# Where the last k features are computed in the prologue of a polysketch attention and squared-ReLU FFN kernel

## Chip, cores, metric

One NeuronCore of a Trainium2 chip. The metric is the device time of one execution in microseconds. Executions come in two states: most agree within 0.3%, a few are 2 to 3.3% longer ("slow").

## The reference, cut to what matters

```python
def phi(x):                                   # per token: 8 x 8 products of two sketches
    a = einsum('rd,bhsd->bhsr', S1, x)        # r = 8, head_dim 32
    b = einsum('rd,bhsd->bhsr', S2, x)
    return einsum('bhsi,bhsj->bhsij', a, b).reshape(..., 64)
q_p, k_p = phi(q), phi(k)                     # batch 4, heads 4, seq 1088
kv  = einsum('bhsf,bhsd->bhfd', k_p, v)
z   = sum(k_p, axis=2)
out = (q_p @ kv) / (q_p . z + 1e-6)           # then x = out as 4352 tokens x 128
h   = relu(x @ w_in)                          # 128 -> 2048
y   = (h * h) @ w_out                         # 2048 -> 128
```

Everything is fp32. The FFN is the bulk of the work. The attention of each batch must be done before that batch's FFN may start, and for the first batch nothing is there to hide it behind. That is the prologue.

## The kernel before

For the first batch the keys are cut into nine tiles of 128 tokens (0 to 8). Each tile goes through three engines:

- `kf`: TensorE computes both sketches of a tile (one matmul per tile, 64 columns) into a PSUM bank;
- `kb`: ScalarE copies one half of it to SBUF;
- `kp`: VectorE multiplies the halves (one instruction per group of tiles);
- `kvp`: TensorE multiplies kp by v and adds up over the tiles (four matmuls per tile, one per head).

The q features of the first 256 tokens take the same way: two sketches `q0(0)` and `q0(1)` on TensorE, the copy `qb` on ScalarE, the product `qp0` on VectorE. When kvp is complete VectorE makes the block `bd` from it, and then den and num (the denominator and the numerator of `out`) and the first FFN input xT follow, after which the FFN matmuls begin.

```python
    def a_kf(t0, n, pool, tag):
        kf = pool.tile([128, 512], F32, tag=tag, name="kf")     # each tag: a ring of two PSUM banks
        for t in range(n):
            nc.tensor.matmul(_ap(kf, 0, 128, 32 * t, [[32 * n, 2], [1, 32]]),
                             kt0[:, 128 * (t0 + t) : 128 * (t0 + t) + 128], sf[:, 0:64])
        kb = wpool.tile([128, 32 * 3], F32, tag="kb", bufs=4, name="kb")
        nc.scalar.copy(kb[:, 0 : 32 * n], kf[:, 32 * n : 64 * n])
        st["kf", t0] = kf, kb
    # ... (a_kp0: one tensor_tensor of kf and kb; a_kv0: four matmuls, 128 rows, 64 columns)
    def q0(x):
        for y in range(2):                                       # two halves of 64 rows
            r, o = slice(64 * y, 64 * y + 64), 512 * (2 * x + y)
            nc.tensor.matmul(x0[:, o : o + 256], sq[r, 128 * x : 128 * x + 128], qT[r, 0:256])
    # ...
    a_kf(0, 2, psf, "po")
    a_kf(2, 2, psf, "pg")
    a_kf(4, 3, psf, "po")
    q0(0)
    q0(1)
    nc.scalar.copy(_ap(qb0, ...), banks(x0, 0, 0, 256))
    st[0, "kvp"] = psf.tile([128, 512], F32, tag="pg", name="kvp")
    for t0, n in ((0, 2), (2, 2), (4, 3), (7, 2)):
        a_kp0(t0, n)
        for t in range(t0, t0 + n):
            a_kv0(t)
        if t0 == 0:
            a_kf(7, 2, psf, "po")
    nc.vector.tensor_tensor(out=_ap(qp0, ...), in0=banks(x0, 2, 0, 256), in1=_ap(qb0, ...), op=mult)
    # ... den0 (eps), bd, kvt, num0, reciprocal, xT, then the FFN
```

Of the kernel before, what the change touches and what calls it, by code (L numbers as in the profile page):

```python
# [14 lines left out]
def _ap(t: bass.AP, p0: int, np_: int, off: int, free):  # L15
    p = list(t.ap)[0]
    return bass.AP(
        t.tensor, t.offset + p0 * p[0] + off, [[p[0], np_]] + [list(d) for d in free]
    )
# [85 lines left out]
def kernel(  # L105
# [43 lines left out]
    psf = ctx.enter_context(tc.tile_pool(name="psf", bufs=2, space=bass.MemoryType.PSUM))  # L149
# [122 lines left out]
    def banks(t_, x, col, n, k=2):  # L272

        return _ap(t_, 0, 128, 512 * x + col, [[512, k], [1, n]])
# [28 lines left out]
    def a_kf(t0, n, pool, tag):  # L303
        kf = pool.tile([128, 512], F32, tag=tag, name="kf")
        for t in range(n):
            nc.tensor.matmul(  # L306
                _ap(kf, 0, 128, 32 * t, [[32 * n, 2], [1, 32]]),
                kt0[:, 128 * (t0 + t) : 128 * (t0 + t) + 128],
                sf[:, 0:64],
# [4 lines that stand above are left out]
# [5 lines left out]
    def a_kp0(t0, n):  # L319

        kf, kb = st["kf", t0]
        nc.vector.tensor_tensor(
            out=_ap(st[0, "kp"], 0, 128, 256 * t0, [[64, 4 * n], [8, 8], [1, 8]]),
            in0=_ap(kf, 0, 128, 0, [[8, 4 * n], [1, 8], [0, 8]]),
            in1=_ap(kb, 0, 128, 0, [[8, 4 * n], [0, 8], [1, 8]]),
            op=mult,
        )
# [45 lines left out]
    def a_kv0(t):  # L373
        for h in range(H):
            i, y, o, o_v = h % 2, h // 2, 64 * (H * t + h), 32 * (NT * h + t)
            nc.tensor.matmul(  # L376
                st[0, "kvp"][64 * i : 64 * i + 64, 64 * y : 64 * y + 64],
                st[0, "kp"][:, o : o + 64],
                _ap(vn[0], 0, 128, o_v, [[VC - o_v, 2], [1, 32]]),
                start=(t == 0 and y == 0),  # L380
                stop=(t == NT - 1),
                skip_group_check=True,
            )
# [362 lines left out]
    def q0(x):  # L746
        for y in range(2):
            r, o = slice(64 * y, 64 * y + 64), 512 * (2 * x + y)
            nc.tensor.matmul(x0[:, o : o + 256], sq[r, 128 * x : 128 * x + 128], qT[r, 0:256])  # L749
# [5 lines left out]
    a_kf(2, 2, psf, "pg")  # L755
    a_kf(4, 3, psf, "po")
    q0(0)
    q0(1)
    nc.scalar.copy(_ap(qb0, 0, 128, 0, [[256, 2], [1, 256]]), banks(x0, 0, 0, 256))
    st[0, "kvp"] = psf.tile([128, 512], F32, tag="pg", name="kvp")  # L760
    for t0, n in ((0, 2), (2, 2), (4, 3), (7, 2)):
        a_kp0(t0, n)
        for t in range(t0, t0 + n):
            a_kv0(t)
        if t0 == 0:
            a_kf(7, 2, psf, "po")
    nc.vector.tensor_tensor(
        out=_ap(qp0, 0, 128, 0, [[256, 2], [1, 256]]), in0=banks(x0, 2, 0, 256),
        in1=_ap(qb0, 0, 128, 0, [[256, 2], [1, 256]]), op=mult,
# [229 lines left out]
    for u in range(NU):  # L999
# [38 lines left out]
        if d0 + m == NB and (b, ci) != (B - 1, last):  # L1038
            po = [x for u_ in range(first_unit[b, c0], u + 1) for x in pe2[u_]]
# [48 lines left out]
```

## Time and profile before

| | before |
|---|---|
| fast runs | 189.06, 189.63 and, profiled, 189.23 us (a fourth, 195.55, was slow) |
| span of the profiled core | 187.4 us |
| first FFN matmul starts | 14.17 us |

Here is the timeline of TensorE in the prologue: start, length, engine (PE is TensorE, PEld its weight loads, DVE VectorE, ACT ScalarE), line, operation, output and inputs, count. TensorE executes in order and the modelled lengths overlap a little, so the cost of a piece is read from its start to the start of the next.

```profile
5.32 1.75 PE L306 MATMUL kf<-sf,kt 128*128 128x64 f32 x14
7.00 1.13 PE L749 MATMUL x<-qT,sq 64*128 64x256 f32 x8
8.06 0.69 PE L376 MATMUL kvp<-vn,kp 128*64 128x64 f32 x16
8.68 0.66 PE L306 MATMUL kf<-sf,kt 128*128 128x64 f32 x4
9.27 1.85 PE L376 MATMUL kvp<-vn,kp 128*64 128x64 f32 x56
11.05 0.65 PE L773 MATMUL den<-eps 1*64 1x256 f32 x4
```

From start to start: both q sketches 1.06 us (7.00 to 8.06), kvp of tiles 0 and 1 0.62, the late kf 0.59, the other kvp 1.78. The sum, from the first sketch to the first den matmul, is 4.05 us. I call this **the stretch**. Every fp32 matmul of this stretch has two records in the trace.

### The profile page before, as it was taken

To read this page: it belongs to the slowest core of one execution; us is meant where nothing else is said; L and a number is where in the kernel's file an instruction comes from. 1 tells how busy PE (TensorE), PEld (TensorE's weight loads), DVE (VectorE), ACT (ScalarE), POOL (GpSimd) and SP (SyncE) were. 2 spreads that over 40 slices of the span, in tenths; PEclk is the share of its full clock that TensorE was granted. 3 is DMA by queue.
4 is the path that set the end of the run, shared out by engine and by line. 5 is a ranking of instruction groups with operands and counts; after the bars stand their busy time and mean duration, and the time that the engine had idled before them with its cause. 6 is when DMAs were issued, how large, how long until landed. Compare 5 with 4: busy or idle time off the path is not lost.

```text
span 187.4 us, 4142 instructions
## 1 busy us (share of the span) xinstructions
PE 182.0 (97%) x1586; PEld 121.8 (65%) x1587; DVE 115.0 (61%) x261; ACT 149.4 (80%) x329; POOL 28.0 (15%) x125
## 2 busy tenths in 40 slices
PE   8999999999999999999999999999999999999991
PEld 2757866666656666656577666656577655666890
DVE  4779879958992589469944589469943412222400
ACT  3418778778978989789698989789698998999960
POOL 2832000028400000085000000085000000000000
PEclk9999999999999999999999999999999999999998
DMA  6799400100039600200069200200020200020101
GB/s 189 189 344 325 125 3 2 28 3 5 0 50 251 143 6 0 44 1 2 7 146 251 35 3 0 42 3 0 7 41 0 35 0 2 9 43 0 31 11 28
DMA packets 24411, 11.27 MB, mean 60 GB/s; under 512 B 17864, under 2 KB 22728, under 8 KB 24392
## 3 DMA queue, kind: packets, MB, share of 16 engines
q1 hardware_dynamic: 23940, 10.82, 23.7%
q8 instruction: 12, 0.20, 0.4%
q10 hardware_dynamic: 452, 0.20, 0.4%
q14 instruction: 7, 0.06, 0.1%
HBM read 8.78 MB, written 2.23 MB: 59 GB/s over the span
## 4 chain that ended last, share of the span: by engine, by line
PE 94%; DMA 2%; DVE 1%; issue 0%; ACT 0%; POOL 0%; ACTq 0%; DVEq 0%
PE po L653 60%; PE pg L615 18%; PE nd L538 3%; PE kvp L394 2%; PE pol L648 2%; PE po L648 2%; PE qc L296 2%; DMA s_nat<-in_S_dram 2%; PE kvp L376 1%; PE kf L306 1%; PE kc L296 1%; PE x L749 1%; PE nd L547 1%; PE den L795 0%; PE den L773 0%
## 5 line engine op out<-in xcount | busy, mean ns | idle before, releaser
L653 PE MATMUL po<-g,w_o 128*128 128x384 f32 (+3 forms) x352 | 138.4, 478 | 0.0
L615 PE MATMUL pg<-xT,w_in 128*128 128x384 f32 (+3 forms) x192 | 110.1, 582 | 0.3 <-DVE xT L810 0.3
L624 ACT ACTIVATE gt<-pg 128x384 f32<-128x384 f32 (+4 forms) x177 | 85.2, 489 | 20.0 <-PE pg L615 16.9
L653 PEld LDWEIGHTS po<-g,w_o 128*128 128x128 f32 x352 | 62.6, 189 | 22.3 <-issue 7.3
L632 ACT ACTIVATE g<-gt 128x384 f32<-128x384 f32 (+3 forms) x138 | 71.0, 532 | 2.9
L615 PEld LDWEIGHTS pg<-xT,w_in 128*128 128x128 f32 x192 | 36.0, 190 | 25.1 <-issue 7.2
L634 DVE TENSOR_TENSOR g<-gt 128x384 f32<-128x384 f32 (+4 forms) x39 | 21.4, 550 | 39.5 <-ACT gt L624 39.4
L443 POOL COPY kv<-kvt 32x64 f32<-32x64 f32 x48 | 11.8, 246 | 89.7 <-PE po L653 63.9
L506 DVE STREAM_SHUFFLE qa<-qc 128x576 f32<-128x576 f32 (+2 forms) x20 | 11.6, 650 | 0.0
L521 DVE TENSOR_TENSOR qp<-qa,qb 128x576 f32<-128x576 f32 (+2 forms) x20 | 10.8, 601 | 0.0
L497 POOL COPY rd<-rc 32x9 f32<-32x9 f32 x48 | 8.9, 185 | 2.2
L347 DVE TENSOR_TENSOR kp<-fs 128x576 f32<-128x576 f32 x12 | 8.2, 741 | 0.0
L469 DVE STREAM_TRANSPOSE qt<-qc 128x576 f32<-128x576 f32 x6 | 4.3, 762 | 5.5 <-PE qc L296 5.5
L657 DVE STREAM_TRANSPOSE oT<-po 128x384 f32<-128x384 f32 (+3 forms) x11 | 6.2, 560 | 1.2 <-PE po L653 1.2
L538 PE MATMUL nd<-qp,kv 32*32 32x288 f32 (+2 forms) x320 | 6.8, 353 | 0.0
L338 DVE STREAM_TRANSPOSE fs<-kc 128x576 f32<-128x576 f32 x6 | 4.3, 762 | 3.9 <-PE kc L296 3.9
L538 PEld LDWEIGHTS nd<-qp,kv 32*32 32x32 f32 x320 | 3.8, 103 | 3.5 <-issue 2.1
L584 DVE TENSOR_TENSOR xT<-nd,bc 128x576 fp32r<-128x576 f32 (+2 forms) x10 | 5.6, 596 | 0.8 <-PE nd L538 0.7
L506 DVE STREAM_SHUFFLE qb<-qc 128x576 f32<-128x576 f32 (+2 forms) x10 | 6.0, 648 | 0.0
L696 PE MATMUL warm<-const-bfloat16-1.0 128*128 128x512 bf16 x12 | 5.2, 585 | 0.8 <-PEq L1072 0.8
L289 DVE STREAM_TRANSPOSE qT<-qn 128x192 f32<-128x192 f32 (+3 forms) x11 | 5.8, 562 | 0.0
L575 DVE STREAM_TRANSPOSE bc<-rd 128x576 f32<-128x576 f32 (+2 forms) x10 | 5.7, 603 | 0.1
(98 smaller groups left out, 97.6 us busy)
## 6 DMA issues: line engine op xcount, KB each, us to landing
kn<-in_k_dram SPq DMA_DIRECT2D x3, 544.0 KB, 6.8
qn<-in_q_dram SPq DMA_DIRECT2D x3, 544.0 KB, 6.7
vn<-in_v_dram SPq DMA_DIRECT2D x9, 144.0 KB, 5.3
out_dram<-oT SPq DMA_DIRECT2D x24, 48.0 KB, 1.8
w_in<-in_moe_w_in_dram SPq DMA_DIRECT2D x4, 256.0 KB, 6.5
w_o<-in_moe_w_out_dram SPq DMA_DIRECT2D x4, 256.0 KB, 5.9
out_dram<-oT SPq DMA_DIRECT2D x8, 56.0 KB, 1.9
qn<-in_q_dram SPq DMA_DIRECT2D x1, 416.0 KB, 5.6
```

The source lines that it names most:

```text
L347: nc.vector.tensor_tensor(out=_ap(st[b, "kp"], 0, 128, 2 * o, [[64, NT], [8, 8], [1, 8]]), in0=_ap(fs, 0, 128, o, [[32, NT], [1, 8], [0, 8]]),
L443: nc.gpsimd.tensor_copy(_ap(st[b, "kv"], 32 * c, 32, 64 * h, [[32, E], [1, 32]]), _ap(st["kvt"], 32 * h, 32, 0, [[64, E], [1, 32]]),)
L497: nc.gpsimd.tensor_copy(st[b, "rd", 0][32 * h : 32 * h + 32, NT * c : NT * c + NT], st[b, "rc"][32 * c : 32 * c + 32, NT * h : NT * h + NT],)
L506: nc.vector.stream_shuffle(in_=banks(st[b, "qc", i0], 2 * x, 0, m), out=_ap(st[b, which, i0], 0, 128, 2 * m * x, [[m, 2], [1, m]]), mask=m ...
L521: nc.vector.tensor_tensor(out=st[b, "qp", i0, e][:, r], in0=st[b, f"qa{e}", i0][:, r], in1=st[b, "qb", i0][:, r], op=mult,)
L538: nc.tensor.matmul(nd[32 * h : 32 * h + 32, 512 * c + col : 512 * c + col + m], kv[r, o : o + 32], qp[r, m * h : m * h + m], start=(e == 0 ...
L615: nc.tensor.matmul(st["pg", u][:, n * i : n * i + n], w_in[:, 128 * (d0 + i) : 128 * (d0 + i) + 128], st[b, "xT"][:, c0 : c0 + n],)
L624: nc.scalar.activation(gt[:, 0:w], st["pg", u][:, 0:w], Relu)
L632: nc.scalar.activation(g2[:, 0:w], gt[:, 0:w], Square)
L634: nc.vector.tensor_tensor(out=g2[:, 0:w], in0=gt[:, 0:w], in1=gt[:, 0:w], op=mult)
L648: nc.tensor.matmul(po[x // 128][:, 0:128], g[:, x : x + 128], w, start=(d == 0), stop=(d == NB - 1),)
L653: nc.tensor.matmul(po[0][:, 0:n], w, g, start=(d == 0), stop=(d == NB - 1))
```

## The change

The k features of tiles 7 and 8 are moved ahead, from between two groups of kvp to between the two q sketches. The intent is visible in the profile: VectorE stands idle for 1.21 us until the copy that follows these features is done.

```diff
     a_kf(4, 3, psf, "po")
     q0(0)
+    a_kf(7, 2, psf, "po")
     q0(1)
     nc.scalar.copy(_ap(qb0, 0, 128, 0, [[256, 2], [1, 256]]), banks(x0, 0, 0, 256))
     st[0, "kvp"] = psf.tile([128, 512], F32, tag="pg", name="kvp")
@@
         a_kp0(t0, n)
         for t in range(t0, t0 + n):
             a_kv0(t)
-        if t0 == 0:
-            a_kf(7, 2, psf, "po")
```

## The prediction

> **What bounds the kernel now.** I read the page first: its engine shares, the 40 slices and the chain that ended last. Then I read the chain piece by piece over the first 25 us, and the timeline of the same stretch for VectorE, ScalarE and GpSimd, because the change touches nothing after about 11 us.
>
> ```profile
> span 187.4 us, 4142 instructions
> PE 182.0 (97%) x1586; PEld 121.8 (65%) x1587; DVE 115.0 (61%) x261; ACT 149.4 (80%) x329; POOL 28.0 (15%) x125
> PE   8999999999999999999999999999999999999991
> PEclk9999999999999999999999999999999999999998
> PE 94%; DMA 2%; DVE 1%; issue 0%; ACT 0%; POOL 0%; ACTq 0%; DVEq 0%
> ```
>
> TensorE is busy 97% of the span, makes 94% of the chain that ended last, and has a full clock in every slice but the last. So the kernel is bound by TensorE's work, from the prologue on. The moved lines stand in slices 2 and 3. The chain there, in order of time (start, length, what):
>
> ```profile
> 5.32 1.75 PE kf L306 x14
> 7.07 1.06 PE x L749 x8
> 8.13 0.61 PE kvp L376 x16
> 8.75 0.59 PE kf L306 x4
> 9.34 1.78 PE kvp L376 x56
> 11.12 0.58 PE den L773 x4
> 11.70 0.61 PE den L795 x4
> 12.33 0.46 DVE dT L804
> ```
>
> Each piece begins where the one before it ended: from 5.32 to 12.33 us the chain never leaves TensorE. The second kf piece (4 records, two matmuls: the k features of token tiles 7 and 8) is what the change moves, from 8.75 to the middle of the x piece (the two q sketches, 7.07 to 8.13). The trace shows two records for each of these fp32 matmuls.
>
> The other engines in the same stretch, from the timeline (start, length, engine, line, what; in brackets the idle time before it and what ended that):
>
> ```profile
> 6.29 2.12 DVE L322 TENSOR_TENSOR kp<-kf,kb 128x512 f32<-128x512 f32 x3
> 8.18 0.59 ACT L759 COPY qb<-x 128x512 f32<-128x512 f32 x1 [0.84 <-PE x L749]
> 9.37 0.21 ACT L312 COPY kb<-kf 128x64 f32<-128x64 f32 x1 [0.61 <-PE kf L306]
> 9.62 0.69 DVE L322 TENSOR_TENSOR kp<-kf,kb 128x512 f32<-128x512 f32 x1 [1.21 <-ACT kb L312]
> 10.23 0.68 DVE L767 TENSOR_TENSOR qp<-x,qb 128x512 f32<-128x512 f32 x1
> 11.17 0.49 DVE L780 TENSOR_TENSOR bd<-kvp,own_p 128x128 f32<-128x128 f32 x2 [0.26 <-PE kvp L376]
> ```
>
> VectorE waits 1.21 us for the last copy kb, and this wait is what the change seems aimed at. But it is off the path: after the last kp (ends 10.31) and the product qp (ends 10.91) VectorE still waits 0.26 us until TensorE has finished kvp.
>
> **What the Trainium skill says, and whether the trace agrees.**
>
> - "PSUM — Partial Sum Buffer", "Engine vs sequencer instructions": ScalarE and VectorE queues are strictly first in, first out, and matmuls start and complete in program order. The trace agrees: qp's input qb was complete at 8.77, yet qp ran only at 10.23, behind the late kp.
> - The same page, "PSUM bank collisions raise a hardware error": an engine's use of a bank has to be guarded by semaphores for the whole bank. The kf of tiles 7 and 8 takes a bank that held the kf of tiles 0 and 1; so it may be written only when ScalarE's copy and VectorE's first kp have read that one. In the trace that first kp runs from 6.29 to about 6.97.
> - "TensorE: Matmul & The Clock Gate", "The mechanism" (Part 3): a weight load overlaps matmuls in flight only where the row groups differ. The q sketches use 64 rows each, kf and kvp all 128. The trace fits: the weight-load row stands idle 0.33 us between the last q sketch and the first kvp, and the first 16 kvp records take 0.61 us (38 ns each) where the later 56 take 1.78 us (32 ns each).
> - The same page, "HAM oscillation — how this bites in real kernels": an idle stretch of over about 3.4 us halves the clock. The longest TensorE wait of the prologue is under 1 us and the change makes none that long, so the clock stays; the PEclk row is the check.
>
> **The change part by part.** Nothing is removed and nothing added: the same two kf matmuls, the same kb copy, the same kp product. By the order of instructions of the two built kernels, four things differ.
>
> 1. TensorE: before, q sketch 0, q sketch 1, kvp of tiles 0 and 1, kf of tiles 7 and 8, kvp of tiles 2 to 8. After: q sketch 0, kf of tiles 7 and 8, q sketch 1, all kvp in a row.
> 2. The moved kf now waits for VectorE's first kp. Before, its semaphore was ScalarE's first kb alone, since the kvp ahead of it had waited for that kp already.
> 3. ScalarE: the last kb comes ahead of the copy qb, so it no longer stands behind it; qb waits for the end of sketch 1, which is now later.
> 4. VectorE: the same order, but qp now has to wait for qb by itself.
>
> The sum on TensorE. Before, from 7.07 to 11.12: 1.06 + 0.61 + 0.59 + 1.78 = 4.04 us. After:
> - sketch 0: half of 1.06 = 0.53;
> - kf, entered from another kind of matmul, as measured: 0.59 (at the 125 ns a record of the first 14, 1.75/14, it would be 0.50);
> - sketch 1: 0.53, and up to 0.10 more for coming back to it;
> - kvp: the first 16 records after a sketch 0.61, the other 56 at the steady rate 1.78, together 2.39.
>
> Sum: 0.53 + 0.59 + 0.53 + 2.39 = 4.04 us. One break (kvp, kf, kvp) is exchanged for another (sketch, kf, sketch). The excess seen at a break in this stretch is about 0.1 us (0.59 against 0.50; 0.61 against 16 x 32 ns = 0.51), so I take 0.0 with an error of 0.2 either way.
>
> The new wait of part 2: the first kp ends about 6.29 + 0.68 = 6.97. The moved kf can reach the array no sooner than 7.07 + 0.53 = 7.60. Even with a hop of 0.14 us (from the first xT's end at 14.03 to TensorE's start at 14.17) the release comes 0.5 us early. No stall.
>
> Side engines: kf ends near 8.2, kb near 8.45, the last kp runs right after the third (8.41) and ends near 9.2, so VectorE's wait shrinks from 1.21 to 0.1 to 0.2 us. Sketch 1 ends near 8.7 instead of 8.13, qb near 9.35, qp near 10.1 instead of 10.91. All this ends before kvp does (11.1), where bd has to wait anyway: 0.8 us of VectorE time gained turns into 0.8 us more waiting for kvp. The last kvp pair of tiles needs the last kp only at 11.12 - 16 x 0.032 = 10.6, and had it at 10.31 before; that slack grows, and it bought nothing.
>
> From bd on, nothing in the program differs. So the whole effect is whatever the 4.04 us turns into, and it can at most shift the rest by that.
>
> **The rivals.**
>
> - *The VectorE wait was on the path* and a good part of 1.21 us is won: 188.1 to 188.5. For: it is the largest VectorE wait of the stretch. Against: the chain has no VectorE piece between 5.32 and 12.33, and bd waits 0.26 us for kvp. I give it 5%.
> - *The breaks are dearer than taken*: splitting the sketches, which run two row halves beside each other, exposes two weight loads of 0.19 us, and the end moves by +0.2 to +0.4: 189.5 to 189.7. For: the 0.33 us of idle weight loads after the sketches. Against: the kf break in kvp cost only 0.09 us. 15%.
> - *One unbroken kvp block is cheaper*: all 72 records at 32 ns are 2.29 instead of 2.39, kf at 0.50: 0.2 us won, 189.1. 25%.
> - *The new bank wait stalls TensorE*: kf, sketch 1 and everything behind it held by kp. Only if kp began 0.5 us later than now. 3%.
> - *The small shift is lost or given back later*, because loads of weights and of q that come later land at times that this does not move. This makes the result still closer to zero.
>
> None reaches 2%, which is 3.8 us: the whole stretch touched is 4.04 us and its TensorE work remains.
>
> **Range and chances.** The kernel before ran at 189.06, 189.63 and, profiled, 189.23; 195.55 is over 1.5% above them and I leave it out as the slow state. Their mean is 189.3. With a shift of 0.0 the prediction is 189.3 us. The spread of runs (0.6 us) and the shift's own error (0.2) give 188.7 to 190.0, 8 times in 10. Faster by 2% needs 185.8: 1%. Slower by 2% needs 193.1, which only the slow state gives: 2%. Within 2%: 97%.
>
> **What would show each step right or wrong.** In the chain after: x, kf x4, x, kvp x72 with no other engine between 5.32 and 12.3, and den L772 (L773 before) beginning at 11.0 to 11.25. In VectorE's timeline: the last kp right behind the other three, no 1.21 us wait, and a wait of about 0.9 us before bd, ended by kvp. The first xT product should start at 13.5 to 13.75 (13.60 before). If bd starts over 0.3 us earlier, VectorE or the breaks counted for more than I think; if the chain shows VectorE's first kp ahead of kf, the bank wait is real. If the first part moves by 0.3 us and the end does not, the later loads set the pace.

## The result, and the profile after

| | before | after |
|---|---|---|
| median of all runs, us | 189.32 (6 runs) | 189.26 (6 runs) |
| ratio after/before | | 0.9998, 95% interval 0.9985 to 1.0012 |
| stretch on TensorE, us | 4.05 | 4.10 |
| VectorE idle ahead of the last kp / of bd, us | 1.21 / 0.26 | 0.16 / 0.94 |
| first FFN matmul starts, us | 14.17 | 14.27 |

A ratio here is the mean time of one kernel's fast runs over the mean of the other's of the same rounds, so it is not quite the ratio of the medians. The two kernels take the same time.

From the page of the kernel after: span, granted clock of TensorE (the share of full speed that it was given) in 40 slices, and the shares of the chain that ended last:

```profile
span 187.5 us, 4142 instructions
...
PEclk9999999999999999999999999999999999999999
...
PE 89%; DMA 6%; SPq 2%; DVE 0%; POOL 0%; issue 0%; ACTq 0%
```

The clock row stayed full. The chain's shares have changed: DMA and its queue now have 8% and TensorE 89%. Experiment e8 below deals with that, because the times do not fit it. TensorE's timeline after the change:

```profile
5.37 1.75 PE L306 MATMUL kf<-sf,kt 128*128 128x64 f32 x14 [0.55 <-ACT sq L717]
7.05 0.70 PE L749 MATMUL x<-qT,sq 64*128 64x256 f32 x4
7.68 0.66 PE L306 MATMUL kf<-sf,kt 128*128 128x64 f32 x4
8.27 0.70 PE L749 MATMUL x<-qT,sq 64*128 64x256 f32 x4
8.90 2.32 PE L376 MATMUL kvp<-vn,kp 128*64 128x64 f32 x72
11.15 0.43 PE L772 MATMUL den<-eps 1*64 1x256 f32 x2
```

Start to start: 0.63 (sketch 0), 0.59 (late kf), 0.63 (sketch 1), 2.25 (all kvp), together 4.10 us. Against before, the sketches went from 1.06 to 1.26 (+0.20), kvp from 2.40 to 2.25 (-0.15), and the late kf kept its 0.59. VectorE's timeline after (in brackets the idle time before and what ended it):

```profile
6.35 2.12 DVE L322 TENSOR_TENSOR kp<-kf,kb 128x512 f32<-128x512 f32 x3
8.62 0.69 DVE L322 TENSOR_TENSOR kp<-kf,kb 128x512 f32<-128x512 f32 x1 [0.16 <-ACT kb L312]
9.64 0.69 DVE L766 TENSOR_TENSOR qp<-x,qb 128x512 f32<-128x512 f32 x1 [0.33 <-ACT qb L760]
11.27 0.49 DVE L779 TENSOR_TENSOR bd<-kvp,own_p 128x128 f32<-128x128 f32 x2 [0.94 <-PE kvp L376]
```

The wait the change was aimed at is gone (1.21 to 0.16 us), a wait of 0.33 us for qb has appeared ahead of qp, as qb now follows a later sketch, and the wait for kvp ahead of bd has grown from 0.26 to 0.94 us. What VectorE gained it waits for TensorE. Last, the weight loads of TensorE after the change:

```profile
7.68 0.52 PEld L306 LDWEIGHTS kf<-sf,kt 128*128 128x128 f32 x4 [0.33 <-DVE kp L322]
...
8.90 0.72 PEld L376 LDWEIGHTS kvp<-vn,kp 128*64 128x64 f32 x22 [0.33 <-issue]
```

The profile says that the moved kf's weight load was idle for 0.33 us until VectorE's kp. If that were so, the new bank wait would be costing time. The same 0.33 us stands ahead of kvp, where it is put down to "issue". Experiment e3 tells which it is.

### The profile page after: what moved, and what is told of

Same layout as the page of the kernel before. It is cut to its first block, busy times and chain, and to the rows that moved or that the text cites. A ratio compares the mean times of both kernels' runs of the same rounds, so it can differ in the third digit from the quotient of the medians.

```text
span 187.5 us, 4142 instructions
## 1 busy us (share of the span) xinstructions
PE 181.7 (97%) x1586; PEld 121.6 (65%) x1587; DVE 115.1 (61%) x261; ACT 149.5 (80%) x329; POOL 28.1 (15%) x125
## 4 chain that ended last, share of the span: by engine, by line
PE 89%; DMA 6%; SPq 2%; DVE 0%; POOL 0%; issue 0%; ACTq 0%
PE po L653 59%; PE pg L615 17%; DMA w_in<-in_moe_w_in_dram 4%; PE nd L538 3%; PE kvp L394 2%; PE pol L648 2%; PE po L648 2%; DMA s_nat<-in_S_dram 2%; PE qc L296 1%; PE kc L296 1%; SPq L200 1%; SPq L191 1%; PE nd L547 1%; SPq L205 1%; POOL w_in L689 0%
## 5 line engine op out<-in xcount | busy, mean ns | idle before, releaser
L648 PE MATMUL pol<-w_o,g 128*128 128x128 f32 x32 | 5.7, 275 | 0.0
```

The costliest lines, as they stand in the source:

```text
L648: nc.tensor.matmul(po[x // 128][:, 0:128], g[:, x : x + 128], w, start=(d == 0), stop=(d == NB - 1),)
```

## The experiments

**Theory.** TensorE's matmuls are the path from the first sketch to bd; VectorE is not. The move exchanges two breaks in TensorE's order: it splits the sketches (+0.20 us) and leaves kvp whole (-0.15 us). What the stretch wins or loses passes to the end.

**Rivals.** (a) The breaks cost nothing and 0.05 us is noise. (b) The new wait for VectorE's first kp holds TensorE and eats a gain. (c) VectorE's wait was on the path, and the gain was lost later. (d) Later DMA loads of w_in absorb any shift, as the chain of after suggests.

All in one table, each with the stretch and the ratio to the kernel before. The last column turns the ratio into microseconds with 189.3 us for the kernel before.

| run | stretch, us | against 4.05 | ratio, 95% interval | in us |
|---|---|---|---|---|
| after | 4.10 | +0.05 | 0.9998 (0.9985 to 1.0012) | -0.04 |
| e1 late kf after both sketches | 3.90 | -0.15 | 0.9989 (0.9976 to 1.0002) | -0.21 |
| e2 late kf first, own bank | 3.76 * | -0.29 | 0.9979 (0.9966 to 0.9992) | -0.40 |
| e3 as after, own bank | 4.11 | +0.06 | 1.0000 (0.9986 to 1.0014) | 0.00 |
| e4 both splits | 4.39 | +0.34 | 1.0012 (0.9997 to 1.0026) | +0.23 |
| e5 before, last kp twice | 4.70 | +0.65 | 1.0025 (1.0011 to 1.0038) | +0.47 |
| e6 after, last kp twice | 4.10 | +0.05 | 0.9996 (0.9983 to 1.0008) | -0.08 |
| e7 tiles 7 and 8 left out | 2.84 | -1.21 | 0.9924 (0.9908 to 0.9939) | -1.44 |
| e8 as after, load order | 4.11 | +0.06 | 0.9996 (0.9981 to 1.0012) | -0.08 |
| e9 late kf first, shared bank | 3.90 * | -0.15 | 0.9989 (0.9975 to 1.0003) | -0.21 |

\* Here the late kf lies ahead of the first sketch, so the time from the first kf matmul to the first den matmul is taken (5.44 and 5.58 us) and 1.68 us is subtracted, which is what the first 14 kf records take before (5.32 to 7.00).

In the profiled runs of e1 and e5 the first 14 kf records took 2.21 and 2.04 us instead of 1.75, so the sketches began 0.42 and 0.28 us later. That lies ahead of the stretch. The traces show the cause: in these two executions the step from one kf record to the next is 0.16 to 0.24 us at first and then 0.11 us, as it is in the other runs, and the trace's entry of the full clock begins at 6.25 us in e1 and at 5.92 in e5, against 4.03 to 5.42 in the other nine. So TensorE began its kf matmuls (5.3 us) on a slower clock there, which the clock row of the page does not show, as the trace has no clock entry before. The profiled execution is also the slowest fast one of e1 (189.46) and of e5 (190.15). One execution can thus be up to 0.4 us late whatever the order, more than most of the effects below. It is why I compare stretches and not points of time.

**e1_kf_after_both.** Neither group is split.

```diff
     q0(0)
     q0(1)
+    a_kf(7, 2, psf, "po")
@@
-        if t0 == 0:
-            a_kf(7, 2, psf, "po")
```

> The late k features (tiles 7 and 8) after both q sketches and ahead of all kvp: no split of the sketches, no split of kvp. I measure the stretch on TensorE from the first kf matmul to the first den matmul: 5.73 us before (5.32 to 11.05), 5.78 us after the change (5.37 to 11.15). Theory (two breaks exchanged: splitting the sketches costs 0.2, leaving kvp whole saves 0.15): stretch 5.59, and the end 0.15 us earlier than before. Rival (a break costs nothing and the 0.05 us of after is noise): stretch 5.7 to 5.8.

TensorE's timeline:

```profile
7.42 1.14 PE L749 MATMUL x<-qT,sq 64*128 64x256 f32 x8
8.48 0.66 PE L306 MATMUL kf<-sf,kt 128*128 128x64 f32 x4
9.07 2.32 PE L376 MATMUL kvp<-vn,kp 128*64 128x64 f32 x72
11.32 0.43 PE L772 MATMUL den<-eps 1*64 1x256 f32 x2
```

The sketches are back at 1.06 us (7.42 to 8.48), kf takes 0.59, kvp stays at 2.25. Stretch 3.90, 0.15 less than before, as expected. (The expected 5.59 counts from the first kf; in this run that count is spoilt by the late start told above.) The end agrees in sign and size, -0.21 us, but its interval just includes no change. So the price of splitting the sketches, with kvp whole in both, is 4.10 - 3.90 = 0.20 us, and the price of splitting kvp, with the sketches whole in both, is 4.05 - 3.90 = 0.15 us.

**e2_kf_first_own_bank.** No break at all: all k features in one run.

```diff
     a_kf(4, 3, psf, "po")
+    a_kf(7, 2, psf, "pg")
     q0(0)
     q0(1)
@@
-        if t0 == 0:
-            a_kf(7, 2, psf, "po")
```

> The late k features directly behind the other k features, ahead of both sketches, in a bank of the other ring, so that no bank wait on the first kp is there. No break at all: theory says stretch 1.68 + 0.50 + 1.06 + 2.25 = 5.49 us, 0.24 less than before, and the end 0.2 us earlier (about 189.1 against 189.3). Rival (the loads or later waits absorb it): stretch 5.49 but the end within 0.1 us of before.

```profile
5.33 2.19 PE L306 MATMUL kf<-sf,kt 128*128 128x64 f32 x18
7.46 1.13 PE L749 MATMUL x<-qT,sq 64*128 64x256 f32 x8
8.52 2.32 PE L376 MATMUL kvp<-vn,kp 128*64 128x64 f32 x72
10.77 0.65 PE L772 MATMUL den<-eps 1*64 1x256 f32 x4
```

From the first kf to the first den matmul 5.44 us against 5.73 (expected 5.49). Four more kf records in the run cost 0.45 us (7.46 - 5.33 - 1.68) where the late kf alone had cost 0.59. This version is the fastest of all: -0.40 us, the interval excludes no change, and the fast runs (188.78 to 188.96) all lie below the fast runs of before of the same call (189.11 to 189.50). It is still only 0.2%.

**e3_kf_between_own_bank.** The changed kernel without the bank wait.

```diff
     q0(0)
-    a_kf(7, 2, psf, "po")
+    a_kf(7, 2, psf, "pg")
     q0(1)
```

> The changed kernel with the late k features in a bank of the other ring: same order of matmuls, but no wait for VectorE's first kp. The profile of after puts the 0.33 us idle weight-load row ahead of the moved kf down to VectorE's kp. Theory (the idle is the end of the sketch's matmuls, whose rows the new weights need): the 0.33 us stays, stretch 5.78. Rival (it is the bank wait): the idle goes, stretch 5.45.

The weight load of the moved kf, to be read beside the line of after:

```profile
7.72 0.52 PEld L306 LDWEIGHTS kf<-sf,kt 128*128 128x128 f32 x4 [0.33 <-issue]
```

The same 0.33 us is there with no wait on VectorE's first kp, now put down to "issue". (In this version kvp takes the bank of the second kf group, which was free long before.) Stretch 4.11, time unchanged. Rival (b) falls: the profile had named the semaphore that the instruction waits on, although it had been given long before (that kp ended at 7.00, the load began at 7.68). I took the idle to come from the sketch's matmuls, which still hold the rows that the new weights need. The 0.33 us is indeed ahead of whatever follows a sketch, in every kernel, but this was not isolated by a run of its own, and it cannot be all: by the records under e4, leaving kf or kvp, which use all 128 rows, costs as much.

**e4_both_splits.** One late kf matmul in each place.

```diff
     q0(0)
-    a_kf(7, 2, psf, "po")
+    a_kf(7, 2, psf, "po", part=0)      # tile 7 only
     q0(1)
@@
         for t in range(t0, t0 + n):
             a_kv0(t)
+        if t0 == 0:
+            a_kf(7, 2, psf, "po", part=1)  # tile 8 into the same bank, then the copy kb
```

> One of the two late kf matmuls between the sketches, the other after the kvp of tiles 0 and 1, into the same tile: both breaks at once. Theory (each break has its own price): 5.78 + 0.15 = 5.93 us stretch, 0.2 over before. Rival (breaks cost nothing): 5.73 to 5.78.

The starts in TensorE's timeline were 6.93 (sketch 0), 7.56 (kf), 7.92 (sketch 1), 8.56 (kvp), 9.17 (kf), 9.54 (kvp) and 11.32 (den). The stretch is 4.39, more than expected. The pieces say why: the sketches cost 0.63 + 0.64 as after the change, kvp 0.61 + 1.78 as before, and the two halves of kf 0.36 + 0.37 = 0.73 instead of 0.59. I had left out that the kf pair itself is split, which costs 0.14. Then it adds up: 3.90 + 0.20 + 0.15 + 0.14 = 4.39. In the stretch, rival (a) falls: each break has a price, and the prices add. The end agrees in sign only (+0.23 us, and the interval includes no change).

The single records show where the price is paid. From the last record of a piece to the first of another kind the step is longer by 0.1 us, whichever kind ends: 0.31 instead of 0.21 us behind a sketch, 0.20 instead of 0.11 behind kf, 0.15 instead of 0.05 behind kvp. The first step inside the new piece is longer too, by 0.05 us (kf, kvp) or 0.10 (sketch). So the changes of kind from the first kf to the first den matmul can be counted: 3 in e2, 4 in e1, 5 before, 5 after and 7 in e4, and the stretches are 3.76, 3.90, 4.05, 4.10 and 4.39 us. The change gained nothing because it left the count at 5. Each kind here uses another shape of the array (kf 128\*128, sketch 64\*128, kvp 128\*64). At the start of the FFN, where pg and po both use 128\*128, the step from pg to po is 0.117 us, no longer than between two pg (0.116 to 0.119). That would fit the shape as the cause; no run tested it alone.

**e5_before_kp_twice and e6_after_kp_twice.** VectorE's last product is done twice, which measures the room that VectorE has in each kernel.

```diff
         a_kp0(t0, n)
+        if t0 == 7:
+            a_kp0(t0, n)
```

> The kernel before with VectorE's last kp product (0.69 us) done twice in a row, same result. It measures the slack of VectorE before bd. Theory (slack 0.26 us ahead of bd and 0.3 us of the last kvp): the second copy ends near 10.92, the last 8 kvp wait for it, bd starts about 11.5 instead of 11.17, and the end is 0.35 us later. Rival (VectorE has a lot of room, or the chain starts elsewhere): no change.

> The changed kernel with the same doubled product. Theory (the change gave VectorE 0.7 us more slack and no time): bd starts where it did, 11.27, VectorE's wait ahead of it shrinks from 0.94 to about 0.4 us, and the end does not move (within 0.1 us of after).

In e5 VectorE comes onto the path. The chain of e5 (start, length, what):

```profile
9.65 0.22 ACT kb L312
...
9.90 0.70 DVE kp L322
...
10.62 0.70 DVE kp L322
...
11.37 0.69 PE kvp L376 x16
```

The last 16 kvp records wait for the second kp and the stretch is 0.65 us longer, the time 0.47. I had expected 0.35, because I took VectorE to have about 0.3 us to spare. It had less: in the kernel before, the last kp ended at 10.31 and the first of the last 16 kvp records started at 10.48. In e5 that record starts at 11.37, counted from the first sketch 0.61 us later than before, and the 16 records then need 0.61 us up to the den matmul (11.98) instead of 0.57. In e6 the same extra work vanishes:

```profile
11.17 0.49 DVE L781 TENSOR_TENSOR bd<-kvp,own_p 128x128 f32<-128x128 f32 x2 [0.63 <-PE kvp L376]
```

The wait ahead of bd went from 0.94 to 0.63 us and neither the stretch nor the time moved. Only 0.31 us of the extra 0.7 shows there, because another part of it filled the wait for qb ahead of qp, which is gone in e6. So the change gave VectorE room and no time. Before, the last kp had 0.17 us to spare (10.31 to 10.48), of which e5 found about 0.1 usable (0.72 us more work came out as 0.61 us of delay); after, it has at least 0.7. Rival (c) falls: the wait of 1.21 us was not on the path, but close to it.

**e7_drop_tiles_7_8.** Wrong result on purpose (relative error 0.068): tiles 7 and 8 left out of the first batch's prologue.

```diff
-    for t0, n in ((0, 2), (2, 2), (4, 3), (7, 2)):
+    for t0, n in ((0, 2), (2, 2), (4, 3)):
@@
-        if t0 == 0:
-            a_kf(7, 2, psf, "po")
```

(and the group's stop flag at tile 6, and the dummy read on GpSimd at the end of tile 6's products)

> Wrong result on purpose: the k features, products and kvp of tiles 7 and 8 are left out of the first batch's prologue. The stretch on TensorE falls by the two late kf matmuls and 16 kvp records, about 0.59 + 0.51 + 0.1 = 1.2 us. If a prologue shift passes to the end: time 1.1 to 1.2 us less (188.1). If later loads (w_in chunk 2 and 3, w_o) absorb it: 0.6 us or less is seen at the end.

The stretch fell by 1.21 us (7.03 to 9.87), the first FFN matmul from 14.17 to 12.99, and the time by 1.44 us (interval 1.15 to 1.74), the profiled span by 1.2 (186.2 against 187.4). A shift of this size in the prologue passes to the end whole, and rival (d) falls for it. For the small shifts the end follows the stretch in sign in e1, e2, e4, e5 and e9, but only for e2 and e5 does the interval exclude no change.

**e8_w_in3_early.** The changed kernel, with the last quarter of w_in loaded one place earlier.

```diff
     load_wi(nc.sync, 2)
-    load_wo(nc.sync, 1)
     load_wi(nc.sync, 3)
+    load_wo(nc.sync, 1)
```

> The changed kernel with the load of the last quarter of w_in issued one place earlier, ahead of the second quarter of w_o. The chain of after names a load of w_in with 4% of the span. Theory (that is a misreading: the matmul at 17.11 waited for ScalarE to free its bank, and the cast only happened to end 0.01 us before): the load lands earlier, the matmul still starts 2.84 us behind the first ffn matmul, time within 0.1 us of after, and w_in is gone from the chain. Rival (the load is on the path): the end moves by 0.1 to 0.4 us.

The shares of the chain in e8:

```profile
PE 94%; DMA 2%; DVE 1%; issue 0%; ACT 0%; POOL 0%; ACTq 0%; DVEq 0%
```

The DMA's 4% for w_in are gone, TensorE is back at 94%, and the time has not moved. In the changed kernel the FFN matmul at 17.11 starts 2.84 us behind the first one at 14.27; in e8, where the last cast of w_in ended at 15.46 instead of 17.09, it starts 2.84 us behind as well (14.30 to 17.14); before, 2.83. So the load was no link of the chain. In the changed kernel the cast happened to end 0.02 us ahead of that matmul, and the profile, which names the latest of the possible releasers, followed it back through 7.5 us of DMA. The kernel before says the same: there this matmul starts at 17.00, 0.36 us ahead of the end of the last cast (17.36). What it waits for was not tried by a run; my guess is ScalarE's ReLU, which has to free the PSUM bank first. The traces of before, after and e8 agree: in each, a ReLU (gt<-pg) ends 0.11 us ahead of that matmul's weight load and releases a semaphore instruction of its line.

**e9_kf_first_shared_bank.** As e2, in the ring that makes the late kf wait for VectorE's first kp.

```diff
-    a_kf(7, 2, psf, "pg")          # e2
+    a_kf(7, 2, psf, "po")          # e9
```

> As the version with the late k features directly behind the others (own bank: stretch 5.44 us from the first kf to the first den matmul, 4.10 with x split, end 0.4 us under before), but in the ring that makes them wait for VectorE's first kp. In the own-bank run that kp ended at 6.99 and the late kf matmuls were due near 7.0. If the bank wait only bites where the order puts the matmul at the moment of the release, it bites here: TensorE's weight load waits on kp, and the stretch is 0.1 to 0.3 us longer than 5.44. Rival (the wait is nothing in any place): 5.44.

```profile
5.32 2.34 PE L306 MATMUL kf<-sf,kt 128*128 128x64 f32 x18 [0.42 <-ACT sq L717]
7.59 1.13 PE L749 MATMUL x<-qT,sq 64*128 64x256 f32 x8
```

The kf run takes 2.27 us to the first sketch (5.32 to 7.59) where it took 2.13 with a bank of its own, and everything behind keeps its length: the stretch is 0.14 us longer, in the range expected, and half of e2's gain is gone. The single records show the wait: kp ends at 6.94 us, the late kf's weight load begins at 7.00, and at the 0.11 us steps of those ahead of it it was due at 6.85. The bank wait is real, but it only bites where the order puts the matmul at the moment of the release. In the change the matmul comes 0.68 us after the release.

## Why the prediction was right

The prediction was 189.3 us in a range of 188.7 to 190.0, and 189.26 was measured. Its steps, one by one:

- *TensorE is the path, VectorE's wait is not.* Right. Shown by e6 (0.7 us more on VectorE costs nothing after the change) and by bd, which waits 0.94 us for kvp where about 0.9 was predicted. But the room before was misread: the last kvp needed the last kp at 10.48 and not at 10.6, so VectorE had 0.17 us to spare and not 0.3 (e5).
- *The sum on TensorE stays at 4.04 us.* Right within its error (4.10), but partly by luck, as the wrong terms cancel. Sketch 0 was put at 0.53 and took 0.63. Sketch 1 was put at 0.53 to 0.63 and took 0.63. kvp was put at 2.39 and took 2.25: I had kept the excess of the first 16 records, which belongs to the break that the change removes. The late kf was put at 0.59 and took 0.59. A break was put at about 0.1 us and costs 0.15 to 0.20, as leaving a kind and entering the next both cost (e4).
- *The row groups.* The prediction read the 38 ns a record of the first 16 kvp, behind a sketch, as a sign of weight loads that cannot overlap. After the change kvp stands behind a sketch too, and its 72 records take 2.25 us, 31 ns each. So that sign was misread. The ends of matmuls are modelled, so these traces do not settle when a weight load overlaps.
- *The rivals.* "The breaks are dearer" and "one unbroken kvp block is cheaper" were given as alternatives. Both were true at once, +0.20 and -0.15 by e1.
- *No stall on the bank.* Right for this order (e3), although the profile of after seems to say the opposite. e9 shows the order in which it would have been wrong.
- *The shift may be lost later.* Not needed: by e7 a shift of 1.2 us passes on whole.
- *What the profile would show.* den began at 11.15 (11.0 to 11.25 predicted), the first xT at 13.70 (13.5 to 13.75), VectorE's wait ahead of the last kp was 0.16 (0.1 to 0.2). The new wait for qb ahead of qp I had put at nothing worth naming; it is 0.33 us and costs nothing. The chain with no other engine between 5.32 and 12.3 did not come true as printed; by e8 that was the page's inference and not the kernel. (A slip without effect: 2% faster than 189.3 us is 185.5, not 185.8.)

A difference of 0.05 us in the stretch is a fortieth of a per cent of the time. The runs cannot see it: the interval of the ratio is 0.27% wide. It is read from the starts in the two traces.

## What to carry to other kernels

Before an engine's wait is attacked, ask what that engine's next consumer waits for: here the idle engine would have waited for TensorE a moment later in any case. Where TensorE is the path and its work is fixed, the order still has a price: matmuls of one kind in one run are cheaper than the same matmuls interleaved (0.14 to 0.20 us for each break here), so count the changes of kind before and after a move; moved work should join its own kind, in a bank that it need not wait for, as in e2. And a releaser in a profile is the latest candidate by the clock: check it against the time at which it was given, and move it in an experiment, before believing it.

## What the Trainium skill lacked or had wrong

- "TensorE: Matmul & The Clock Gate", "The mechanism", says when a weight load can overlap matmuls in flight, and "TensorEngine Tiling (Array Packing)", "Key Properties", that a change of the tiling mode drains TensorE; neither gives a time for what a change of kind costs. Here leaving a kind of fp32 matmul costs 0.1 us and entering the next 0.05 to 0.10; splitting the sketches in two costs 0.20 us, splitting the kvp matmuls 0.15, splitting a kf pair 0.14.
- "PSUM — Partial Sum Buffer", "PSUM bank collisions raise a hardware error", gives the rule to guard by bank and no hint of what the guard costs. Here it was 0 or 0.14 us for the same pair of matmuls, by their place in the order (e3, e9).
- No page found has the second state of a program on one core: executions of 194.4 to 195.6 us (kernel before) beside 189.3 us, at a granted clock of 0.995 to 1.0 in the records. Its cause stays open.
